# Retention, Mish MLP and GLU on one core: the round's loads are asked for behind a four-byte transfer out of that round's state copy

## The chip, the core and the metric

The kernel runs on one core of one Trainium2 chip. The metric is the device time of one execution in microseconds; the median of several runs is compared.

## What is computed

Three stages follow each other, all in float32. The first is a retention (linear attention with decay) over 2 batches of 768 tokens with 8 heads of 64; the other two are MLPs over the resulting 1536 tokens of width 512.

```python
for t in range(S):
    state = gamma * state + einsum('bhd,bhe->bhde', k[:, :, t], v[:, :, t])
    y[:, :, t] = scale * einsum('bhd,bhde->bhe', q[:, :, t], state)
x = y as (1536, 512)
h = x @ w_in                 # 512 -> 2048
x = (h * tanh(softplus(h))) @ w_out
out = (sigmoid(x @ w_gate) * (x @ w_val)) @ w_out2   # 512 -> 1536 -> 512
```

## The kernel before, in words

The retention is computed in chunks of 128 tokens: six chunks for each of two batches, so 12 rounds (`NSUB`). Each round needs two loads of 512 KB from HBM: `qk_t` (q and k of the chunk, features on the partitions) and `nv_t` (k and v of the chunk, tokens on the partitions). Both come from a pool of four buffers per kind (`AHEAD = 4`, line 774), so a load of a later round waits until the round four before has read its buffer for the last time. `load_qk` and `load_nv` (lines 787 to 795) issue them on SyncE.

From round 5 on, the loop at line 1017 runs `block(j)` (line 934). On TensorE a block holds the state products and half of the scores of round j+1, beside the second half of the outputs of round j-1, then the first half of the outputs of round j with the rest of the scores and of the state of round j+1. Between them stand `keep(j+1, 0)` and `keep(j+1, 1)` (line 860): ScalarE (ACT) copies the running state from PSUM into a tile `s` from a pool of six buffers. The second of them writes `s_t[2 * j + 4]` and is the last thing that `block(j)` issues. `at_prep(j+2)` (line 801) multiplies v by the decay on GpSimd (POOL) into `vp`; it is the first reader of `nv_t` of round j+2. The first reader of `qk_t` of round j+1 are the scores at the start of `block(j)`.

Behind `block(j)` the loop asks for `nv_t` of round j+4 and `qk_t` of round j+3, calls `feed()`, which decodes a weight piece and asks for the next one (`load_piece`, line 356: 512 KB into one of two `raw` buffers, which come free when DVE has decoded them), and then runs a few parts of the first MLP (`work`, line 964) so that TensorE stays busy between blocks. Those are the matmuls `h<-xc`, `hx<-xc`, `h<-B` and `hx<-B` of the trace. In rounds 8 and 9 a `put_block` on ScalarE stands in the middle of the block (line 1016), and in round 8 there is no `feed()`.

In this early part every engine's queue keeps the order in which the program issues (`Queue.issue`, line 143: each instruction is placed after the last one of its engine). SyncE's queue holds all the loads of this part, in order, but for five small tables that ScalarE asks for at the start. After the retention (line 1036 on) a planner, `replay()`, sets the order of the rest from modelled costs; the early part is not in its plan. Because all of it is issued by one helper, nearly all instructions have line 147 in the profile, and they are told apart by their tiles: `sc` scores, `st` state, `ao` outputs of the retention, `s` the state copies, `raw` weight pieces.

Of the kernel before, what the change touches and what calls it, by code (L numbers as in the profile page):

```python
# [9 lines left out]
F32 = mybir.dt.float32  # L10
# [8 lines left out]
P = 128  # L19
# [4 lines left out]
def kernel(ctx, tc, qk, nv, w1i, w1o, w2g, w2v, w2o, ma_in, og_in, sg_in, ck_in, mh_in, out):  # L24
# [12 lines left out]
    NSUB = qk.shape[0]  # L37
# [13 lines left out]
    AHEAD = 4  # L51
# [123 lines left out]
    sync = Queue(nc.sync, lambda n, kw: 1.4 if isinstance(kw["out"], Part) else 1.6, 3.5)  # L175
# [279 lines left out]
    def flush():  # L455
        flush_hi()
        while late_lo:
            late_lo.pop(0)()
        fresh.clear()
# [286 lines left out]
    def run(*parts):  # L746
        for p in parts:
            for s in p:
                s()
# [22 lines left out]
    with ExitStack() as actx:  # L772
        ac = actx.enter_context(tc.tile_pool(name="ac", bufs=1))
# [8 lines left out]
        ck = ac.tile([P, SPB, 2 * NP, 1], F32, name="ck")  # L782
        sg = ac.tile([P, SPB, NP, 1], F32, name="sg")
        og_t = [ac.tile([P, NP, P], F32, name=f"og{b}") for b in range(SPB)]
        qk_t, nv_t, a_t, vp_t, st_t, s_t, sc_t, o_t = {}, {}, {}, {}, {}, {}, {}, {}

        def load_qk(j):
            if j < NSUB:
                qk_t[j] = ld.tile([P, 2, NP, P], F32, tag="qk", name="qk_t")
                sync.dma_start(out=qk_t[j], in_=qk[j])  # L790

        def load_nv(j):
            if j < NSUB:
                nv_t[j] = ld.tile([P, 2, 2 * NP, D], F32, tag="nv", name="nv_t")
                sync.dma_start(out=nv_t[j], in_=nv[j])
# [5 lines left out]
        def at_prep(j):  # L801
            if j >= NSUB:
                return
            vp_t[j] = at3.tile([P, 2 * NP, D], F32, tag="vp", name="vp")
            pool.tensor_tensor(
                out=vp_t[j], in0=nv_t[j][:, 1], in1=ck[:, j % SPB].to_broadcast([P, 2 * NP, D]), op=ALU.mult
            )
            if 0 < j < T:
                decays(j)
# [10 lines left out]
        def scores(j, r):  # L820

            if j >= NSUB:
                return []
            sc, t = ps_h.tile([P, 2, NP, Q], F32, tag="h", name="sc"), qk_t[j]
            sc_t[j, r] = sc

            def pair(p):
                for s in range(2):
                    quarter(sc[rows(s), p // 2, 2 * (p % 2) + (r + p) % 2, :], t[rows(r), 1, p, rows(s)],
                            t[rows(r), 0, p, rows(s)])  # L830

            return [lambda p=p: pair(p) for p in range(NP)]

        def mask(j):
            if j >= NSUB:
                return
            a_t[j] = a = at.tile([P, 2, NP, P], F32, tag="a", name="a")[:, :, :, :Q]
            for r in range(2):
                h = slice(r, NP - r, 3 - 2 * r)
                dve.tensor_tensor(out=a[:, :, h], in0=sc_t.pop((j, r))[:, :, h, :],  # L840
                                  in1=mh.to_broadcast([P, 2, NP // 2, Q]), op=ALU.mult)

        def state(j, s):

            if j >= NSUB:
                return [lambda: [quarter(st_t[0][rows(c), 0, :], z[rows(0), rows(0)], z[rows(0), rows(0)]) for c in range(2)]]
            v, k = vp_t[j], nv_t[j]
            new = j % SPB == 0 and s == 0
            if new:
                st_t[0] = ps_s.tile([P, NP, D], F32, tag="s", name="st")  # L850
            st = st_t[0]

            def pair(p):
                for e in range(2):
                    quarter(st[rows((e + p) % 2), p, :], k[rows(s), 0, 2 * p + e, :], v[rows(s), 2 * p + e, :],
                            new and p == 0, p == NP - 1)

            return [lambda p=p: pair(p) for p in range(NP)]

        def keep(j, s):  # L860
            s_t[2 * j + s + 1] = at6.tile([P, NP, D], F32, tag="s", name="s")
            act.activation(out=s_t[2 * j + s + 1], in_=st_t[0], func=AF.Copy)

        def outs(j, row):

            if not T <= j < NSUB:
                return []
            if row == 0:
                o_t[j] = ps_o.tile([P, NP, P], F32, tag="o", name="ao")
            a, v, t, o = a_t[j], vp_t[j], qk_t[j], o_t[j]  # L870

            def inside(p):
                for e in range(2):
                    quarter(o[rows(e), p, rows(row)], v[rows(row), 2 * p + e, :], a[rows(row), p // 2, 2 * (p % 2) + e, :],
                            row == 0 and p == 0, False)

            def across(p, s):
                for m in range(2):
                    quarter(o[rows((row + m) % 2), p + m, rows(s)], s_t[2 * j + s][rows(row), p + m, :],
                            t[rows(row), 0, p + m, rows(s)], False, True)  # L880

            return [lambda p=p: inside(p) for p in range(NP)] + [
                lambda p=p, s=s: across(p, s) for s in range(2) if (2 * j + s) % (2 * SPB) for p in (0, 2)]
# [44 lines left out]
        def lanes(*sides):  # L928
            for n in range(max(map(len, sides))):
                for side in sides:  # L930
                    if n < len(side):
                        side[n]()

        def block(j, middle=lambda: None):

            lanes(state(j + 1, 0) + scores(j + 1, 0), outs(j - 1, 1))
            if True:
                b = (j - 1) // SPC, (j - 1) % SPC * P
                dve.tensor_tensor(out=acc_t[b[0]][:, :, b[1]:b[1] + P], in0=o_t[j - 1], in1=og_t[(j - 1) % SPB], op=ALU.mult)
            if j == NSUB:  # L940
                return
            keep(j + 1, 0)
            flush()
            at_prep(j + 2)
            middle()
            while late_g:
                late_g.pop(0)()
            if j < NSUB - 1:
                lanes(outs(j, 0), scores(j + 1, 1) + state(j + 1, 1))
                mask(j + 1)  # L950
            else:
                run(outs(j, 0), state(j + 1, 1))
            keep(j + 1, 1)
# [10 lines left out]
        def work(n):  # L964
            for _ in range(n):
                dense.pop(0)()

        def feed():
            pump()
            load_piece()  # L970
# [45 lines left out]
        middles = {2 * SPC: lambda: put_block("B11", 1, 0), 2 * SPC + 1: lambda: put_block("B21", 1, 2)}  # L1016
        for j in range(T + 1, NSUB + 1):
            block(j, middles.get(j, lambda: None))
            load_nv(j + AHEAD)
            load_qk(j + AHEAD - 1)  # L1020
            if j < NSUB and j != 2 * SPC:
                feed()
            if j == NSUB:
                flush()
            for n in range(SHARE[j - T]):
                if j == NSUB:
                    lo_eng["g"] = dve if n > 2 else pool
                    run(late_g)
                    late_g.clear()
                work(1)  # L1030
# [114 lines left out]
```

## Time and profile before

| | |
|---|---|
| median of 3 runs | 580.72 us (578.43 to 580.99) |
| the profiled execution's own time | 578.88 us |
| its span, first to last instruction | 577.0 us |
| TensorE (PE) busy | 568.1 us, 98% of the span |
| VectorE (DVE) busy | 458.9 us, 80% |
| ScalarE (ACT) busy | 294.4 us, 51% |
| GpSimd (POOL) busy | 219.1 us, 38% |
| granted TensorE clock | 1.000 |
| HBM read, written | 48.63 MB, 3.15 MB |
| loads of qk_t and of nv_t | 12 each, 512 KB, 6.7 and 6.8 us to landing (median) |
| loads of raw | 68, 512 KB, 3.2 to 3.4 us to landing (median) |

Shares are of the whole span, and the span has unlike parts: the retention takes the first 66 us, the two MLPs the rest. "Time to landing" runs from the start of a DMA's issue on its queue to the arrival of its last byte's signal. Matmuls overlap in the engine's pipeline, so busy times of TensorE say whether it was ever without work, not how fast it ran.

### The profile page before, as it was taken

What the parts mean: (1) busy time and instruction counts of PE and PEld (TensorE: products, weight loads), DVE (VectorE), ACT (ScalarE), POOL (GpSimd) and SP (SyncE); (2) the same over time, 40 slices, a digit from 0 to 9 for tenths busy, and PEclk for the clock granted to TensorE, in tenths of its full rate; (3) what the DMA queues carried; (4) which work ended last, traced back from release to release, by engine and by line L of the source; (5) the groups of instructions that cost most, each with busy time, mean ns of one, the idle gap of its engine ahead of it and who ended that gap; (6) DMA issues with size and microseconds to landing.
All of it is one profiled execution on the core that took longest, in us unless ns stands there. A gap on an engine that the chain in (4) does not pass through costs nothing.

```text
span 577.0 us, 9810 instructions
## 1 busy us (share of the span) xinstructions
PE 568.1 (98%) x3880; PEld 479.2 (83%) x3880; DVE 458.9 (80%) x680; ACT 294.4 (51%) x544; POOL 219.1 (38%) x198
## 2 busy tenths in 40 slices
PE   8899999999999999999999999999999999999997
PEld 6777888888888888888888878888888888888885
DVE  3877599898998787778988888789888788775574
ACT  1566677585645545355665677545346254231210
POOL 3455588533522300024597554423245043020000
PEclk9999999999999999999999999999999999999999
DMA  9984202422332222112100233221322222000014
GB/s 344 404 294 159 76 0 74 136 86 77 105 110 73 74 73 74 37 39 108 37 1 0 91 128 111 74 87 59 110 74 73 74 73 74 1 0 2 0 38 181
DMA packets 15741, 52.40 MB, mean 91 GB/s; under 512 B 2128, under 2 KB 2256, under 8 KB 15696
## 3 DMA queue, kind: packets, MB, share of 16 engines
q1 hardware_dynamic: 14976, 51.39, 25.5%
q8 instruction: 30, 0.49, 0.3%
q10 hardware_dynamic: 720, 0.40, 0.2%
q14 instruction: 15, 0.12, 0.1%
HBM read 48.63 MB, written 3.15 MB: 90 GB/s over the span
## 4 chain that ended last, share of the span: by engine, by line
PE 95%; DMA 3%; DVE 1%; issue 0%; POOL 0%; SPq 0%; ACT 0%; POOLq 0%; DVEq 0%
PE h L147 37%; PE o L147 37%; PE hx L147 17%; DMA nv_t<-nv 3%; PE ao L147 2%; PE st L147 1%; PE sc L147 1%; DVE h L147 0%; POOL vp L147 0%; SPq L147 0%; DVE acc L147 0%; DVE ww L147 0%; ACT e L147 0%; POOLq L147 0%; DVEq L147 0%
## 5 line engine op out<-in xcount | busy, mean ns | idle before, releaser
L147 PE MATMUL o<-g,wo 128*128 128x512 f32 x492 | 119.1, 391 | 0.0
L147 DVE TENSOR_TENSOR acc<-o,acc 128x512 f32<-128x512 f32 x126 | 86.9, 690 | 39.5 <-PE o L147 37.7
L147 PE MATMUL o<-wo,g 128*128 128x512 f32 x432 | 108.6, 392 | 0.0
L147 PEld LDWEIGHTS o<-g,wo 128*128 128x128 f32 x492 | 90.3, 188 | 17.4
L147 PE MATMUL h<-B,ww 128*128 128x512 f32 x372 | 94.4, 390 | 0.0
L147 PE MATMUL h<-T,ww 128*128 128x512 f32 x366 | 92.9, 390 | 0.1
L147 PEld LDWEIGHTS o<-wo,g 128*128 128x128 f32 x432 | 78.5, 189 | 14.7 <-DVE g L147 0.3
L147 PEld LDWEIGHTS h<-T,ww 128*128 128x128 f32 x366 | 68.4, 188 | 15.1 <-ACT e L147 0.5
L147 PEld LDWEIGHTS h<-B,ww 128*128 128x128 f32 x372 | 68.9, 188 | 13.9
L147 DVE SCALAR_TENSOR_TENSOR raw<-raw 128x512 int32<-128x512 int32 x68 | 61.9, 912 | 2.2 <-ACT raw L147 2.0
L147 ACT ACTIVATE raw<-raw 128x512 int32<-128x512 uint8 x68 | 45.6, 670 | 34.3 <-DMA raw<-w2v 9.1
L147 DVE SCALAR_TENSOR_TENSOR v<-v,raw 128x512 int32<-128x512 int32 x68 | 58.5, 865 | 3.1 <-ACT v L147 0.8
L147 PE MATMUL hx<-xc,ww 128*128 128x256 f32 (+1 forms) x342 | 58.3, 307 | 0.0
L147 POOL TENSOR_TENSOR ww<-s,ww 128x512 fp32r<-128x512 f32 x22 | 30.1, 1371 | 67.8 <-ACT ww L147 67.8
L147 PEld LDWEIGHTS hx<-xc,ww 128*128 128x128 f32 x342 | 50.6, 190 | 5.4 <-DVE ww L147 0.3
L147 POOL TENSOR_TENSOR wo<-v,wo 128x512 fp32r<-128x512 f32 x16 | 21.1, 1330 | 86.2 <-ACT wo L147 49.7
L147 DVE TENSOR_TENSOR h<-h,u 128x512 f32<-128x512 f32 x54 | 37.6, 697 | 15.9 <-PE h L147 14.9
L147 ACT ACTIVATE e<-h 128x512 f32<-128x512 f32 x29 | 17.3, 596 | 59.4 <-PE h L147 48.2
L147 ACT ACTIVATE v<-raw 128x512 f32<-128x512 f32 x68 | 45.1, 666 | 2.1 <-POOL wo L147 1.2
L147 PEld LDWEIGHTS hx<-YT,ww 128*128 128x128 f32 x270 | 38.3, 190 | 3.5
L147 PE MATMUL hx<-YT,ww 128*128 128x256 f32 x270 | 39.4, 282 | 0.0
L147 ACT ACTIVATE g<-h 128x512 fp32r<-128x512 f32 x53 | 31.4, 597 | 14.9 <-DVE h L147 13.9
(97 smaller groups left out, 836.4 us busy)
## 6 DMA issues: line engine op xcount, KB each, us to landing
raw<-w1i SPq DMA_DIRECT2D x16, 512.0 KB, 3.3
raw<-w1o SPq DMA_DIRECT2D x16, 512.0 KB, 3.4
qk_t<-qk SPq DMA_DIRECT2D x12, 512.0 KB, 6.7
nv_t<-nv SPq DMA_DIRECT2D x12, 512.0 KB, 6.8
raw<-w2g SPq DMA_DIRECT2D x12, 512.0 KB, 3.2
raw<-w2v SPq DMA_DIRECT2D x12, 512.0 KB, 3.3
raw<-w2o SPq DMA_DIRECT2D x12, 512.0 KB, 3.3
out<-acc SPq DMA_DIRECT2D x12, 256.0 KB, 2.0
```

Of the source, the lines that this page charges most:

```text
L147: i = call(**kw)
```

## The change

A tile `mark` of 12 floats per partition is added to the pool of the retention. In rounds 5 to 8, ahead of the round's loads, SyncE issues a transfer of one float from the state copy that `block(j)` made last into one column of `mark`. Nothing reads `mark`. SyncE must wait for the copy before it issues that transfer, and its queue keeps order.

```diff
--- before.py
+++ after.py
@@ -782,6 +782,7 @@
         ck = ac.tile([P, SPB, 2 * NP, 1], F32, name="ck")
         sg = ac.tile([P, SPB, NP, 1], F32, name="sg")
         og_t = [ac.tile([P, NP, P], F32, name=f"og{b}") for b in range(SPB)]
+        mark = ac.tile([P, NSUB], F32, name="mark")
         qk_t, nv_t, a_t, vp_t, st_t, s_t, sc_t, o_t = {}, {}, {}, {}, {}, {}, {}, {}
 
         def load_qk(j):
@@ -1016,6 +1017,8 @@
         middles = {2 * SPC: lambda: put_block("B11", 1, 0), 2 * SPC + 1: lambda: put_block("B21", 1, 2)}
         for j in range(T + 1, NSUB + 1):
             block(j, middles.get(j, lambda: None))
+            if j + AHEAD - 1 < NSUB:
+                sync.dma_start(out=mark[:1, j:j + 1], in_=s_t[2 * j + 4][:1, 0, :1])
             load_nv(j + AHEAD)
             load_qk(j + AHEAD - 1)
             if j < NSUB and j != 2 * SPC:
```

## Rows read from the trace of the kernel before

**Rows 1.** Busy time by stretch: us, busy time and instructions by engine, clock, DMA

```profile
28.00:48.00 20.00, 19.47 (x563) 15.15 (x562) 15.34 (x25) 13.31 (x28) 10.29 (x9) 1.00 0.87 305
48.00:66.00 18.00, 17.06 (x376) 14.13 (x376) 12.39 (x17) 11.77 (x24) 8.37 (x7) 1.00 0.31 102
66.00:577.00 511.00, 507.10 (x2523) 429.96 (x2521) 414.83 (x608) 259.92 (x475) 189.00 (x169) 1.00 0.20 66
```

**Rows 2.** The chain of waits from 28 to 66 us, by line, and one piece

```profile
by line: PE hx L147 26.1%; PE h L147 24.8%; PE ao L147 22.0%; PE st L147 12.4%; PE sc L147 7.0%; issue 4.5%; DVE ww L147 2.3%; DVE acc L147 1.2%; DVEq L147 0.1%
...
48.00 0.73 issue
```

**Rows 3.** The timeline of SyncE's queue, 29 to 45 us: start, length, transfer

```profile
29.10 0.33 SPq L147 DMA_DIRECT2D raw<-w1i  x1
29.52 0.38 SPq L147 DMA_DIRECT2D nv_t<-nv  x1
30.00 0.38 SPq L147 DMA_DIRECT2D qk_t<-qk  x1
34.05 0.33 SPq L147 DMA_DIRECT2D raw<-w1o  x1
...
35.30 0.33 SPq L147 DMA_DIRECT2D qk_t<-qk  x1
...
39.63 0.37 SPq L147 DMA_DIRECT2D nv_t<-nv  x1
40.06 0.42 SPq L147 DMA_DIRECT2D qk_t<-qk  x1
...
44.54 0.33 SPq L147 DMA_DIRECT2D qk_t<-qk  x1
```

**Rows 4.** DMA issues in short windows around single requests of rows 3: us to landing

```profile
raw<-w1i SPq DMA_DIRECT2D x1, 512.0 KB, 3.3
...
nv_t<-nv SPq DMA_DIRECT2D x1, 512.0 KB, 5.6
...
qk_t<-qk SPq DMA_DIRECT2D x1, 512.0 KB, 6.4
...
qk_t<-qk SPq DMA_DIRECT2D x1, 512.0 KB, 6.0
...
nv_t<-nv SPq DMA_DIRECT2D x1, 512.0 KB, 6.1
...
qk_t<-qk SPq DMA_DIRECT2D x1, 512.0 KB, 7.0
```

**Rows 5.** The timelines of TensorE and GpSimd: the first readers of the moved loads

```profile
39.05 0.23 PE L147 MATMUL sc<-qk_t 64*64 64x64 f32 x2
...
43.45 0.28 PE L147 MATMUL sc<-qk_t 64*64 64x64 f32 x4
...
48.85 0.27 PE L147 MATMUL sc<-qk_t 64*64 64x64 f32 x2
...
52.96 0.26 PE L147 MATMUL sc<-qk_t 64*64 64x64 f32 x2
...
49.19 1.04 POOL L147 TENSOR_TENSOR vp<-nv_t,ck 128x512 f32<-128x512 f32 x1 [0.83 <-POOL g L147]
```

**Rows 6.** The timeline of ScalarE: the second state copy of rounds 5 to 8

```profile
30.90 0.38 ACT L147 ACTIVATE s<-st 128x256 f32<-128x256 f32 x1 [0.33 <-PE st L147]
...
36.23 0.39 ACT L147 ACTIVATE s<-st 128x256 f32<-128x256 f32 x1
...
40.80 0.38 ACT L147 ACTIVATE s<-st 128x256 f32<-128x256 f32 x1 [0.63 <-PE st L147]
...
46.85 0.36 ACT L147 ACTIVATE s<-st 128x256 f32<-128x256 f32 x1
```

**Rows 7.** What SyncE's queue waited for, 28 to 66 us: us, times, longest

```profile
SPq L147 <- DVE v L147: 55.0, 8, 22.7
```

**Rows 8.** The tile view of qk_t over the whole span: time to landing

```profile
DMA to landing us min/median/max: 3.5/6.7/9.1
```

## The prediction

> **What bounds the kernel now.** I first read the stretches of the span. From 66 us on the attention part is over; TensorE is busy 507.10 of 511 us at full granted clock and the DMA engines are 0.20 busy [rows 1]. Nothing the change touches runs there. The four new transfers belong to rounds 5 to 8, between about 29 and 48 us. In that stretch TensorE is busy 19.47 of 20.00 us and the DMA engines 0.87; in the tail of the attention, 48 to 66, TensorE is busy 17.06 of 18.00 and the DMA engines 0.31 [rows 1]. So TensorE sets the pace there too, and the loads run beside it: heavy traffic, but nobody waits for it.
>
> The second view is the chain of waits over 28 to 66 us. No transfer is on it. What is not TensorE's own work is "issue" with 4.5% of 38 us (1.7 us), DVE ww with 2.3% (0.9 us) and DVE acc with 1.2% (0.5 us) [rows 2]. A change in load times can take time out only by removing part of these 3.0 us, and can add time only by making a load land after its first use. The third reading therefore sets, for each moved load, request, landing and first use side by side [rows 3 to 5].
>
> **The change, part by part.**
>
> *The wait.* SyncE issues in order, so a transfer that waits for the round's second state copy holds back all that follows. The copies end at 30.90+0.38 = 31.28, 36.62, 41.18 and 47.21 us [rows 6]. SyncE reached the same place earlier, at 29.52 in round 5 and at 39.63 in round 7 (round 6 lies between, with its qk request at 35.30), so the wait is real each time [rows 3]. The new transfer's own issue is not in the trace; the other issues take 0.33 to 0.42 us with gaps near 0.1 [rows 3], so I take 0.33 and put the first load 0.5 us behind the copy's end, the second 0.4 behind that. New requests: nv 31.8, 37.1 and 41.7; qk 32.2, 37.5 and 42.1; in round 8, which has no nv load left, qk at 47.7. The seven loads are nv 9 to 11 and qk 8 to 11. The qk requests come 2.2, 2.2, 2.0 and 3.2 us later than 30.00, 35.30, 40.06 and 44.54 [rows 3], the nv requests 2.3 us (29.52) and 2.1 us (39.63) later.
>
> *What else is behind it on SyncE.* The weight loads. They wait for a free raw buffer, that is for the decode on DVE: 55.0 us of waiting over eight requests [rows 7]. The one after round 5 is asked for at 34.05, while the held pair would be out by 32.6; rounds 6 and 7 repeat this. I cost the delay of weight loads at nothing; the cover is DVE's decode, and if that came 1.4 us earlier the weight load would start behind the pair in sequence anyway, as now.
>
> *The four-byte transfer itself.* Nobody reads its target. The state copy's buffer is written again six copies later, so the copy at 46.85 [rows 6] would be the first to wait for the transfer issued at 31.3. Its time to landing is not in the trace: from above I bound it with a whole 512 KB load, 3.3 us [rows 4], so it is done by 35; from below it is nothing. Neither end touches the sum. ACT gets perhaps one more semaphore to test on three copies; ACT idled 0.33 us before one such copy [rows 6], and I take nothing.
>
> *The loads' landing.* Before, request plus time to landing gives qk 36.4 (30.00+6.4), 41.3, 47.1 and 50.5 (6.0 holds for both the second and the fourth), and nv 35.1 (5.6) and 45.7 (6.1) for the first and the last [rows 3, 4]. First uses on TensorE are 39.05, 43.45, 48.85 and 52.96; nv's latest margin is on POOL at 49.19 [rows 5]. The margins are thus 2.6, 2.1, 1.8 and 2.5 us for qk and 3.5 us for the last nv. The two ends:
>
> - Upper end: the delay passes to the landing in full, as if the load took as long as before. qk lands at 38.6, 43.5, 49.1 and 53.7, that is 0.45 us early, then 0.05, 0.25 and 0.75 us late. A late load moves later requests and later uses alike, so these add up to at most 1.05 us.
> - Lower end: a load with nothing in front of it lands 3.3 us after its request [rows 4]. The request at 31.8 then lands at 35.1, where it lands now, and qk 1.3 us behind it (the distance now, 35.1 to 36.4) at 36.4, as now. A transfer asked for later finds less in front of it. Lateness is zero. Below that a gain is possible: traffic that stands clear of other fetches for two microseconds per round could remove stalls without a visible cause, the largest of which is 0.73 us at 48.00 [rows 2]. At most the whole 1.7 us of "issue".
>
> I take the lower end without a gain, because the first pair's landing follows from the nearest row (a weight load of equal size, 3.3 us, in the same stretch at 29.10), and because traffic in the round stage is below full, 0.87 [rows 1], so that a 2 us hole can be refilled.
>
> The rows show landings in the order of requests, with 1.3 to 1.4 us between an nv and its qk [rows 3, 4]. The Trainium skill, in "DMA: Bandwidth & Descriptors", section "Rules for kernel authors", says to issue a transfer early and wait for it late, so that its fixed cost lies beside compute. By that rule the change goes the wrong way and the sum would be the upper end, 1.05 us. The margins above are measured and larger than or nearly equal to the delays, so I let the margins decide.
>
> *Sum:* 0 (wait, covered by 1.8 to 3.5 us of margin) + 0 (weight loads) + 0 (four transfers) = 0 us, with ends at -1.7 and +1.05. The profiled execution took 578.88 us on a span of 577.0; the sum leaves 578.9 there. The median of the three runs is 580.72, 1.8 above, and the runs spread from 578.43 to 580.99. Against the median: 580.7.
>
> **The rivals.**
>
> *Loads become the pace (slower).* If the time to landing were that of the crowded start, up to 9.1 us for qk [rows 8], qk would be needed 6.85, 5.95, 6.75 and 5.25 us after its new request and come 2.25, 3.15, 2.35 and 3.85 us late. Because two rounds overlap, each lateness also relaxes the next deadline: the totals grow 2.25, 3.15, 4.6, 7.0. The price is 7.0 us, 587.7. It decides from a time to landing above 5.3 us in round 8 and 6.0 in round 6. For it: the margins of 1.8 to 2.6 us are about as large as the delay, and TensorE's queue is in order, so that late scores stop everything. Against it: the start is crowded because requests pile up; here the queue is drained when the request comes, so 3.3 to 5 us is more like it. Chance of more than 2.9 us: 0.07.
>
> *Delay passes in full (the upper end).* The load takes as long as before from a later request: 580.7+1.05 = 581.8, no visible difference. For it: the times to landing hardly vary, 5.6 to 7.0 us, whatever was asked before [rows 4]. Against it: those loads each stood behind another one, which the wait undoes. Chance 0.20. (It is also where the skill's rule above would lead; no run here shows it yet.)
>
> *The hole in the traffic pays (faster).* All of the 1.7 us of "issue" going gives 579.0, still within the bound. With DVE ww and acc too (3.0 us) it would be 577.7, 0.5% faster. For it: the 0.73 us stall falls while the queue is loaded. Against it: the held loads are moved into later, equally loaded microseconds, their bytes do not shrink; and DVE's part has no transfer as its releaser. Chance of a visible gain: 0.07; of a gain below it, 0.18.
>
> *The change holds nothing back.* If the copies were done before SyncE arrived, all would stay as it is, 580.7. The rows speak against it in all four rounds. Chance 0.03.
>
> **How the numbers follow.** My forecast, no difference, has 0.45; the upper end 0.20, the small gain 0.18 and the idle change 0.03 also lie within 0.5% (2.9 us, about what a measurement of this kernel can tell from no change). That makes same 0.86, faster 0.07, slower 0.07. The range takes in the small gain and the spread of the runs below (580.7-1.7-1.0 = 578.0) and, above, the late loads with the same 1.0 and a little of the slow rival: 583.0.
>
> **What would show it.** Right: SyncE's nv and qk requests near 31.8/32.2, 37.1/37.5, 41.7/42.1 and 47.7, each about 0.5 us behind the end of a state copy; times to landing of 3.5 to 5 us in place of 5.5 to 7; first scores of the rounds within 1 us of 39.05, 43.45, 48.85 and 52.96; weight requests where they were. Wrong: TensorE idle before scores or POOL idle before vp with a load as the releaser; the last part of the attention, up to 66 us, longer or shorter by over 2 us; or any change in the stretch after 66 us, for which I have no mechanism.

## The result, and the profile after

The change makes the kernel slower. Its median is 584.43 us (581.34 to 587.38, 15 runs) against 580.93 us before (578.43 to 584.16, 15 runs): a ratio of 1.0059, 95% interval 1.0037 to 1.0080. A second measurement of the same two kernels, among the experiments below, gave 1.0039 (1.0022 to 1.0056). No difference was forecast, at 580.7 us in a range of 578.0 to 583.0.

The profiled execution after took 582.36 us on a span of 580.6; the one before 578.88 on 577.0. Both lie near the fast end of their kernel's runs, so they show one part of the difference well and, as will be seen, not all of it.

First the busy time by stretch, after (columns as in [rows 1]).

```profile
28.00:48.00 20.00, 16.85 (x520) 13.31 (x522) 12.51 (x20) 10.82 (x22) 9.25 (x8) 1.00 0.80 261
48.00:66.00 18.00, 16.49 (x390) 13.47 (x379) 13.79 (x21) 12.52 (x26) 8.35 (x6) 1.00 0.36 121
66.00:580.00 514.00, 510.35 (x2567) 432.49 (x2565) 416.09 (x610) 261.59 (x478) 190.43 (x170) 1.00 0.21 67
```

Against [rows 1], TensorE works 16.85 us of the 20 us between 28 and 48, where it worked 19.47. Its totals over the span agree to 0.1 us (568.1 before, 568.2 after), so nothing was added to its work: it stood still. In the stretch from 66 us on it is busy 510.35 of 514 us, as before 507.10 of 511. The clock is 1.00 throughout. The whole loss of this execution arose between 28 and 66 us.

The chain of waits of 28 to 70 us, after, names what stood still.

```profile
by line: PE h L147 24.6%; PE hx L147 23.6%; PE ao L147 19.3%; PE st L147 11.2%; issue 10.9%; PE sc L147 5.5%; DVE ww L147 2.3%; ACT g L147 1.3%; ACT ww L147 1.2%; ACT s L147 0.9%
...
39.28 1.50 issue
...
45.28 1.46 issue
...
49.95 0.29 issue
...
50.92 0.46 issue
...
55.22 0.76 issue
```

"Issue" has 10.9% of 42 us, 4.6 us; before it had 4.5% of 38 us, 1.7 us [rows 2]. Five pieces carry it; the one of 0.29 us stands before too, at 47.03, ahead of the same matmul. No load is on the chain, neither nv nor qk. So TensorE waited for something, at four places, that the profile does not tie to a semaphore, and the difference of 2.9 us is most of the 3.6 us that the span grew.

SyncE's queue, after, is what the prediction asked to see first.

```profile
31.18 0.72 SPq L147 DMA_DIRECT2D mark<-s  x1
32.01 0.34 SPq L147 DMA_DIRECT2D nv_t<-nv  x1
32.45 1.06 SPq L147 DMA_DIRECT2D qk_t<-qk  x1
33.98 0.33 SPq L147 DMA_DIRECT2D raw<-w1o  x1
36.57 0.60 SPq L147 DMA_DIRECT2D mark<-s  x1
37.27 0.33 SPq L147 DMA_DIRECT2D nv_t<-nv  x1
37.70 0.41 SPq L147 DMA_DIRECT2D qk_t<-qk  x1
...
42.77 0.59 SPq L147 DMA_DIRECT2D mark<-s  x1
43.46 0.33 SPq L147 DMA_DIRECT2D nv_t<-nv  x1
43.89 0.39 SPq L147 DMA_DIRECT2D qk_t<-qk  x1
...
50.16 0.58 SPq L147 DMA_DIRECT2D mark<-s  x1
50.84 0.34 SPq L147 DMA_DIRECT2D qk_t<-qk  x1
```

The hold works as intended: the pair of rounds 5 and 6 is asked for at 32.01/32.45 and 37.27/37.70, where 31.8/32.2 and 37.1/37.5 were forecast, and the weight load at 33.98 is where it was [rows 3]. The four-byte transfers take SyncE 0.58 to 0.72 us to issue, where 0.33 was taken. From round 7 on all requests are later than forecast, because TensorE had already stopped at 39.28.

Were the loads late? The times to landing of the four held qk loads, after, in the order of their requests:

```profile
qk_t<-qk SPq DMA_DIRECT2D x1, 512.0 KB, 5.4
...
qk_t<-qk SPq DMA_DIRECT2D x1, 512.0 KB, 6.2
...
qk_t<-qk SPq DMA_DIRECT2D x1, 512.0 KB, 6.6
...
qk_t<-qk SPq DMA_DIRECT2D x1, 512.0 KB, 3.8
```

By request and time to landing they land near 37.9, 43.9, 50.5 and 54.6 us. The rows of TensorE around the first stall, after (start, length, operation, and in brackets the idle time before it):

```profile
38.98 0.23 PE L147 MATMUL sc<-qk_t 64*64 64x64 f32 x2
...
39.06 0.22 PE L147 MATMUL ao<-qk_t,s 64*64 64x64 f32 x1
40.78 0.21 PE L147 MATMUL ao<-qk_t,s 64*64 64x64 f32 x1 [1.50 <-issue]
```

The first scores of round 7's block run at 38.98, over a microsecond after qk had landed, and TensorE then stops for 1.50 us in the middle of a series of like matmuls whose operands are all there. The same in the next two blocks, where the first scores run at 45.00, ahead of the stall, and at 51.50, behind it and 1.0 us after the load:

```profile
45.00 0.28 PE L147 MATMUL sc<-qk_t 64*64 64x64 f32 x4
46.74 0.27 PE L147 MATMUL ao<-qk_t,s 64*64 64x64 f32 x2 [1.46 <-issue]
...
51.37 0.33 PE L147 MATMUL ao<-a,vp 64*64 64x64 f32 x3 [0.46 <-issue]
51.50 0.27 PE L147 MATMUL sc<-qk_t 64*64 64x64 f32 x2
```

What the stalls have in common is their place in the instruction stream. Counted in the trace they lie 254 recorded TensorE instructions apart (matmuls and weight loads), in the kernel before as in the changed one. Before they end at 43.82, 48.73 and 52.79, after at 46.74, 51.37 and 55.98, at the same instructions; the largest one after, which ends at 40.78, has no counterpart before. The chain before, beside the 0.73 us at 48.00 of [rows 2]:

```profile
43.73 0.09 issue
...
52.57 0.21 issue
```

Part 3 of the profile's page shows what comes in such portions: queue 8, kind "instruction", moved 0.49 MB in 30 packets, 16 KB each, and TensorE ran 7760 matmuls and weight loads, 259 for each packet. The Trainium skill, in "Runtime: NRT & Kernel Launch", section "Instruction fetch mechanics", says the same of an engine's program: it is refilled in blocks of 16 KiB, 256 instructions, by DMA. It adds that the cost of such a block's end is mostly hidden; in this stretch the trace does not agree, it costs up to 1.50 us at a time. To keep them apart from the kernel's `block(j)`, these blocks of the program are called portions below; the expectations call them pages, and the DMA engines' queues rings.

The fetch that ends the first stall can be placed with narrow windows. The DMA queues of 36.8 to 37.0 us, before (packets, MB, share of 16 engines):

```profile
q8 instruction: 1, 0.02, 28.7%
```

and of 38.5 to 38.7 us, after:

```profile
q8 instruction: 1, 0.02, 30.6%
```

It is one packet that holds one DMA engine for about 1 us (30.6% of 16 engines over 0.2 us is 0.98 us). Up to 38.9 us TensorE stands at the same instructions in both traces to within 0.1 us, yet the fetch begins at 36.87 before and at 38.58 after, 1.7 us later. It ends at 39.56, and TensorE goes on at 40.78. In all profiles of this study TensorE goes on 1.1 to 1.7 us after such a fetch has ended; where the end of the portion is reached later than that, there is no stall.

### The profile page after: what moved, and what is told of

Its sections match the earlier page's. It is cut to its first block, busy times and chain, and to the rows that moved or that the text cites. A ratio compares the mean times of both kernels' runs of the same rounds, so it can differ in the third digit from the quotient of the medians.

```text
span 580.6 us, 9824 instructions
## 1 busy us (share of the span) xinstructions
PE 568.2 (98%) x3880; PEld 479.2 (83%) x3880; DVE 458.8 (79%) x680; ACT 294.4 (51%) x544; POOL 219.5 (38%) x198
## 4 chain that ended last, share of the span: by engine, by line
PE 94%; DMA 3%; issue 1%; DVE 1%; ACT 0%; ACTq 0%; POOL 0%; POOLq 0%; SPq 0%; DVEq 0%
PE h L147 37%; PE o L147 36%; PE hx L147 17%; DMA nv_t<-nv 2%; PE ao L147 2%; DMA sg<-sg 1%; PE st L147 1%; PE sc L147 0%; DVE h L147 0%; ACTq L147 0%; POOL vp L147 0%; DVE ww L147 0%; DVE acc L147 0%; ACT e L147 0%; ACT g L147 0%
## 5 line engine op out<-in xcount | busy, mean ns | idle before, releaser
L147 ACT ACTIVATE raw<-raw 128x512 int32<-128x512 uint8 x68 | 45.5, 670 | 37.5 <-DMA raw<-w2v 10.7
L147 PEld LDWEIGHTS hx<-xc,ww 128*128 128x128 f32 x342 | 50.5, 190 | 5.4 <-DVE ww L147 0.3
```

The lines of the kernel that those rows point to most:

```text
L147: i = call(**kw)
```

## The experiments

The theory after the first profile: the hold brings the loads into the way of TensorE's instruction fetches (fetch theory). Its rivals: the loads land too late for their readers (late-load theory), and the four-byte transfers themselves disturb (transfer theory). Ratios are to the kernel before, with 95% intervals.

| run | ratio | interval |
|---|---|---|
| e1 transfer behind the first state copy | 1.0001 | 0.9982 to 1.0020 |
| e2 the change, 64 instructions more at the start | 1.0082 | 1.0053 to 1.0111 |
| e3 the change, loads in halves | 1.0107 | 1.0080 to 1.0135 |
| e4 hold in rounds 5 and 6 alone | 1.0013 | 0.9998 to 1.0029 |
| f1 hold in rounds 7 and 8 alone | 1.0030 | 1.0011 to 1.0048 |
| f2 before, 64 instructions more at the start | 1.0054 | 1.0035 to 1.0073 |
| f3 the change, two weight loads one round later | 1.0037 | 1.0015 to 1.0058 |
| f4 before, two weight loads one round later | 0.9978 | 0.9960 to 0.9996 |
| g1 before, 64 instructions more in rounds 1 and 2 | 1.0062 | 1.0046 to 1.0077 |
| g2 the change, the same | 1.0107 | 1.0090 to 1.0124 |
| g3 before, three more loads, no hold | 1.0005 | 0.9991 to 1.0020 |
| g4 as f4, and one part of the MLP earlier | 0.9965 | 0.9949 to 0.9981 |
| h1 the change again | 1.0039 | 1.0022 to 1.0056 |
| h2 hold in round 7 alone | 1.0035 | 1.0016 to 1.0053 |
| h3 the change with the edits of g4 | 1.0034 | 1.0013 to 1.0055 |

**e1: the transfers without the hold.**

```diff
-                sync.dma_start(out=mark[:1, j:j + 1], in_=s_t[2 * j + 4][:1, 0, :1])
+                sync.dma_start(out=mark[:1, j:j + 1], in_=s_t[2 * j + 3][:1, 0, :1])
```

> The four transfers stand where they stand in the change, but read the round's first state copy (ends 29.5, 35.2, 39.7 and 44.1 us in the trace before), so that SyncE is held by 0 to 1 us instead of 2 to 3. Fetch theory (the held loads get in the way of TensorE's instruction fetches, which then come 1.7 to 2.8 us later, and TensorE runs dry): the loads are back within 1 us of their old requests, the stalls called issue between 28 and 66 us fall from 4.6 back to 1.7 to 2.5 us, ratio 0.999 to 1.002. Transfer theory (the four-byte transfers themselves disturb the rings or SyncE): they are all still there, stalls stay near 4.6 us, ratio 1.005 to 1.007.

Measured: 579.97 us, ratio 1.0001. All four transfers are there, only what they wait for comes earlier. The transfer theory falls: four issues and four bytes cost nothing that can be measured. The cost is in the hold. Its profile has 2.4 us of issue between 28 and 70 us (0.63, 0.30, 1.28 and 0.22), the upper end of what was expected. The profiled execution was the slowest of the twelve, 583.40 us, with a stretch at half clock ahead of the rounds, so that its stalls need not be those of the median.

**e4, f1 and h2: which rounds.** The condition ahead of the transfer becomes `j < 7` (e4), `6 < j and j + AHEAD - 1 < NSUB` (f1), or:

```diff
-            if j + AHEAD - 1 < NSUB:
+            if j == 7:
```

> The four-byte transfer in rounds 5 and 6 alone. Fetch theory: the first big stall (1.50 us at 39.3, fetch at 38.6 behind the loads of rounds 5 and 6) stays, the second (1.46 us at 45.3, fetch at 44.3 behind round 7's held pair) goes: ratio 1.002 to 1.004. Late-load theory (round 8 has the least margin, rounds 5 and 6 the most): no loss, 0.999 to 1.001.

> The four-byte transfer in rounds 7 and 8 alone. Rounds 5 and 6 alone cost 0.1%. If the cost sits where the margin of the loads is least and the traffic fullest (both theories): most of the loss, ratio 1.003 to 1.006. If the cost needs the whole row of holds, each pushing the next: 1.001 to 1.003. Fetch theory: the stall of 1.5 us at 39.3 is gone, one of about 1.5 us near 44 to 45 (behind the pair of round 7) stays. Late-load theory: no big stall before 47, then a wait that ends on qk 10 (scores near 48.9).

> The four-byte transfer in round 7 alone. Rounds 7 and 8 cost 0.30%. In their profile the fetch behind round 7's pair came at 51.1 and TensorE stood 2.1 us at 51.5. If that is where the cost sits: ratio 1.002 to 1.004, a stall of 1.5 us or more between 47 and 53 us. If it is round 8's held qk: 0.999 to 1.001.

Measured: 1.0013, 1.0030 and 1.0035. Rounds 5 and 6 cost next to nothing by themselves; the expected stall of 1.5 us at 39.3 did not come in e4's profile, nor one near 44 to 45 in f1's, which has its own of 2.10 us at 51.47. The profiles of e4, f1 and h2 have a stretch at half clock ahead of the rounds, and TensorE comes to round 5 about 3 us later than before; their stalls can't be set place by place against those of the change's first profile. Round 7 alone costs as much as rounds 7 and 8 together, and as much as the whole change in its second measurement. That is neither what the late-load theory says (round 8 has the least margin to its load) nor what the prediction's upper end says (0.25 us for round 7).

The profile of h2 shows how round 7's hold does it. SyncE's queue:

```profile
44.34 0.72 SPq L147 DMA_DIRECT2D mark<-s  x1
45.17 0.34 SPq L147 DMA_DIRECT2D nv_t<-nv  x1
45.60 0.37 SPq L147 DMA_DIRECT2D qk_t<-qk  x1
46.42 0.33 SPq L147 DMA_DIRECT2D raw<-w1o  x1
```

The pair is held to 45.17 and 45.60, until round 7's last state copy, and the weight load follows at 46.42, so that 1.5 MB are asked for within 1.6 us, ahead of the time when TensorE reaches the end of round 8's block, near 48.5 us. The fetch for the next instructions then begins here, in the window 50.9 to 51.1:

```profile
q8 instruction: 1, 0.02, 29.8%
```

and TensorE has its first matmul behind the end of its instructions at 53.24:

```profile
53.24 0.33 PE L147 MATMUL ao<-a,vp 64*64 64x64 f32 x3 [2.10 <-issue]
```

Before, the fetch of the same instructions began 0.9 us after the end of that block (45.4), in the window 46.2 to 46.4:

```profile
q8 instruction: 1, 0.02, 30.2%
```

So the same fetch comes about 2.5 us behind the block's end in place of 0.9, with the same loads in front of it, but asked for later. Round 8's block is followed by one of the two shortest dense pieces (two parts of the first MLP, 1.6 us), so that the next block, 256 recorded instructions in 2 to 3 us, comes soon.

**e2, f2, g1 and g2: the same instructions in other places of their portions.** e2 and f2 add 16 tiny warm-up matmuls, g1 and g2 put as many matmuls of zeros into rounds 1 and 2; e2 and g2 start from the change, f2 and g1 from the kernel before.

```diff
             pe.matmul(out=o, lhsT=z[:, 0:P], rhs=z)
+        for n in range(16):
+            pe.matmul(out=o[:, 0:Q], lhsT=z[:, 0:P], rhs=z[:, 0:Q])
```

```diff
             at_state(j)
+            for n in range(8 if 0 < j < 3 else 0):
+                quarter(st_t[0][rows(0), 0, :], z[rows(0), rows(0)], z[rows(0), rows(0)], False, False)
```

> The change, with 16 more tiny warm-up matmuls at the start of TensorE's queue, 64 instructions, which lie in its idle start. Fetch theory: every page of 256 instructions ends 64 instructions earlier in the program, so the stalls leave the places where they stand now (after the second to fourth retention outputs of the blocks of rounds 7 and 8) and reappear 64 instructions earlier, in front of the blocks or in their first state products; their sizes change, because the fetches meet other loads: ratio anywhere between 0.998 and 1.008. Late-load theory (TensorE waits for qk or nv that come too late): the stalls stand before the same matmuls as now, ratio 1.005 to 1.007.

> The kernel before, with the same 16 tiny warm-up matmuls (64 instructions). Fetch theory: its small stalls (0.73 us at 48.00, 0.21 at 52.57, 0.09 at 43.73) go from their places and come 64 instructions earlier or nowhere; no hold, so no load is late: ratio 0.997 to 1.002, and the loss of the change against it is the late loads' part. If the warm-up itself costs (2 us at the start that are not hidden): 1.002 to 1.004.

> The kernel before, with 16 tiny matmuls that add zeros to the state (64 TensorE instructions) in rounds 1 and 2, where the start waits for its loads anyway. The same shift of the page ends as with the longer warm-up, without its start cost of about 1 us. Fetch theory: the small stalls leave 48.00 and 52.57; from the run with the longer warm-up one of 1.7 us is to be expected near 46 to 47, in the dense matmuls: ratio 1.001 to 1.005. If the position of the instructions in their pages does not matter: 0.999 to 1.001.

> The change with the same 64 instructions in rounds 1 and 2. Fetch theory: the stalls of 1.5 us at 39.3 and 45.3 go, others come, as with the longer warm-up: ratio to before 1.004 to 1.009. Late-load theory (the position in the pages does not matter): stalls as in the change, 1.005 to 1.007, before the same matmuls.

Measured: 1.0082, 1.0054, 1.0062 and 1.0107. The two stalls of the change at 39.3 and 45.3 are gone in e2, as the fetch theory says, and its largest one, 2.59 us at 50.91, stands 64 instructions ahead of the place of the change's stall at 55.22, among the last products of round 9's block (chain of waits):

```profile
50.91 2.59 issue
```

In f2 the stall of the kernel before at 48.00 has moved to 46.98, into the dense matmuls, with 1.72 us; g1 and g2 stop at that same instruction, for 2.05 us (at 49.05) and 3.09 us (at 50.38). The position of the instructions in their portions decides where TensorE stops; the late-load theory has no room for that. But the times are no clean measure, and all four lie above what was expected, e2 by very little: the 64 instructions were not hidden. In f2 the rounds begin about 1 to 2 us later than before, in g1 about 3 us (the weight load of 29.10 is asked for at 31.01 and at 32.12), a large part of what these kernels lose (3.1 and 3.6 us). What can be read from the pairs is the hold's price on other bases: 0.3% between f2 and e2, which their intervals do not clear of zero, and 0.45% between g1 and g2, which theirs do.

e2 also shows how a late load appears in a trace. TensorE's row in round 9's block:

```profile
49.29 0.27 PE L147 MATMUL sc<-qk_t 64*64 64x64 f32 x2 [0.87 <-DMA qk_t<-qk]
```

Here the wait ends on qk itself and the profile says so: 0.87 us. In the two profiles of the change no such row exists. The late-load theory names a limit that is close by, about 1 us away, but not the one that was met.

**e3: loads in halves.**

```diff
-                sync.dma_start(out=qk_t[j], in_=qk[j])
+                for h in halves(j):
+                    sync.dma_start(out=qk_t[j][h], in_=qk[j][h])
...
-        sync.dma_start(out=t, in_=src[kind][i])
+        for h in ((slice(0, Q), slice(Q, P)) if early and n > 2 else (slice(0, P),)):
+            sync.dma_start(out=t[h, :], in_=src[kind][i][h])
```

`nv` is treated as `qk`; `halves(j)` gives two halves of 64 partitions from chunk 8 on.

> The change, with the loads of rounds 5 on (nv and qk from chunk 8, raw from piece 3, in the early part) asked for as two halves of 64 partitions. Fetch theory, if a fetch waits for the share of whole transfers in front of it: half the wait, the stalls called issue fall from 4.6 to 2 to 3 us, ratio 1.001 to 1.004. If a fetch waits for all that is asked for: no change, 1.005 to 1.007. Late-load theory: more issues on SyncE (0.33 us each), later landings, 1.006 to 1.010.

Measured: 1.0107, a miss for the fetch theory's first form. Stalls of 2.24 us (at 53.40) and 1.12 us remain, and a wait for qk joins them. Counted from 128 recorded instructions ahead of the portion's end, a mark that all traces share, the fetches for the places of the change's first three stalls began after 2.2, 2.8 and 3.9 us, against 3.1, 2.5 and 1.4 us in the change's first profile: on the whole they did not get their turn sooner behind shorter transfers. But e3 also doubles the issues on SyncE, so its time is not the halves' effect on fetches alone. What a fetch waits for, whether all that has been asked for or something else, stays open. The Trainium skill, in "DMA: Bandwidth & Descriptors", section "Queues, rings and completion order", says that each DMA engine takes turns between its queues packet by packet; by that rule, if one transfer's share of an engine makes a packet, halves should have helped, and they did not.

**f3, f4, g4 and h3: less traffic in the same stretch.** The weight loads of rounds 6 and 7 are asked for one round later (f3 on the change, f4 on the kernel before). g4 and h3 also move one part of the first MLP from behind round 11 to behind round 9.

```diff
-            if j < NSUB and j != 2 * SPC:
-                feed()
+            if j == T + 2:
+                pump()
+            elif j == 2 * SPC:
+                load_piece()
+            elif j < NSUB:
+                feed()
```

```diff
-    SHARE = (4, 4, 3, 3, 2, 2, 4, 5, 5)
+    SHARE = (4, 4, 3, 3, 2, 3, 4, 4, 5)
```

> The change, with the weight loads of rounds 6 and 7 asked for one round later (behind the loads of rounds 7 and 8; they are decoded at 50.8 and 55.8 us in the trace before, so they have the time). One transfer of 512 KB less between 39 and 48 us. Theory that full rings behind the held pair delay fetches and qk: ratio 1.002 to 1.004, qk 9 and 10 land 1 us or more sooner after their request (5 us or less instead of 6.2 and 6.6), the stall at 45.3 shrinks below 1 us, the one at 39.3 stays. If the hold costs by itself, whatever the traffic: 1.005 to 1.007.

> The kernel before, with the weight loads of rounds 6 and 7 asked for one round later. If TensorE's stalls between 43 and 53 us (1.0 us in all) come from full rings: they halve, ratio 0.997 to 0.999. If they do not depend on the traffic: 1.000. If the later weight pieces come too late for the decode: 1.001 to 1.004.

> The kernel before with the weight loads of rounds 6 and 7 one round later (0.998 by itself) and one part of the first MLP moved from behind round 11 to behind round 9, so that TensorE has dense work while a fetch is under way. Fetch theory: the stall near 52 to 54 (0.3 to 0.7 us) goes too: ratio 0.996 to 0.999. If the moved part only shifts work: 0.998, as without it.

> The change with the weight loads of rounds 6 and 7 one round later and one part of the first MLP moved from behind round 11 to behind round 9 (0.9965 without the hold). If the hold's cost is the fetches behind the held pairs: it stays about 0.5% above that kernel, 1.000 to 1.004, with a stall near 50 us. If thin traffic makes up for the hold: 0.996 to 0.999.

Measured: 1.0037, 0.9978, 0.9965 and 1.0034. Thinner traffic makes the kernel before 0.2% faster. With the hold it shows no clear gain: f3's 1.0037 stands against 1.0059 and 1.0039 for the change, and its profile has 2.38 us of stall at 50.00 and none at 39.3, where one was expected to stay. With the MLP part g4 is the fastest kernel of the study, 578.82 us against 581.22 on its chip. Its chain between 28 and 70 us:

```profile
by line: PE h L147 33.6%; PE hx L147 24.6%; PE ao L147 17.1%; PE st L147 11.9%; PE sc L147 5.7%; issue 2.6%; POOL og L147 2.4%; DVE ww L147 2.2%; DVE acc L147 1.1%; POOLq L147 0.1%
...
43.87 0.26 issue
...
47.33 0.30 issue
...
52.49 0.30 issue
```

Issue is down to 2.6% of 42 us, 1.1 us, and the 0.73 us at 48.00 [rows 2] is gone. The hold keeps its price: 0.6% between f4 and f3, 0.7% between g4 and h3. h3's profile still has stalls of 1.08 and 1.17 us (at 44.52 and 54.77; near 50, where one was expected, it has 0.46). So the traffic of the two weight loads is not what makes the hold dear; what is left is the time at which the pair is asked for.

**g3: more traffic without a hold.**

```diff
             load_qk(j + AHEAD - 1)
+            if j < 2 * T:
+                sync.dma_start(out=acc_t[2][:, 0:2, :], in_=qk[j].rearrange("p a b c -> p a (b c)"))
```

> The kernel before, with one more load of 512 KB behind the pair in rounds 5 to 7 (three in all; it writes a part of the accumulator that is overwritten later, so it adds traffic only). No load is held. Fetch theory: TensorE's stalls at the ends of its pages grow (1.0 us in all between 43 and 53 us before) to 3 us or more, though the pairs are asked for when they were: ratio 1.003 to 1.010. Late-load theory: TensorE waits at the scores for qk, and the chain shows the load as releaser: 1.002 to 1.008. If neither the fetches nor the loads are near their limit: 0.999 to 1.001.

Measured: 1.0005, no difference, although its profile shows what the fetch theory expects:

```profile
by line: PE hx L147 24.6%; PE h L147 23.4%; PE ao L147 20.2%; issue 11.9%; PE st L147 11.2%; PE sc L147 6.4%; DVE ww L147 2.5%; DVE acc L147 1.1%; DVEq L147 0.1%
...
39.70 1.43 issue
...
45.62 1.25 issue
...
51.05 1.28 issue
```

With no load held, three more loads on the DMA engines put TensorE's stalls at the same three instructions as in the change, 1.43, 1.25 and 1.28 us, with no load as releaser. That supports the mechanism. The ratio does not follow, a miss: 4 us of stalls in one profile, and 0.05% in the medians. Two things lie between. The first is that the stalls differ from run to run. Five profiles, of kernels without added matmuls, have no stretch at half clock up to 570 us: before, after, g3, g4 and h3. Their spans are 577.0, 580.6, 580.4, 576.3 and 579.8 us, their "issue" between 28 and 70 us is 1.7, 4.6, 5.0, 1.1 and 3.4 us, and the span less this issue is 575.2 to 576.4 us in all five. By this estimate an execution at full clock is slower by about as much as its stalls are longer. So the profile before, 578.88 us, shows less stall time than the median of its kernel has, and that of g3, the second slowest of its twelve runs (582.23 us against a median of 581.44), shows more. At full clock the medians of g3 and of the kernel before on its chip are 581.2 and 580.7 us, a difference that is not clear of noise. The second is that ten of the twelve runs of g3 are at full clock, which leads to the last question.

**h1: the change again, with the clock of every run.** No edit.

> The change, unaltered, to see a second profile and the clock of every run of both kernels on one chip. If the loss is only the stalls that the first profile shows at full clock (4.6 us of issue against 1.7): the runs at full clock of both kernels differ by 3 to 3.5 us, and lower clocks are as frequent in both. If stalls also bring the clock down: runs at full clock differ by 1 to 2.5 us, most runs of the change are below full clock and a third or fewer of those of before, and a profile at a lower clock shows the fall right behind a stall of 2 us or more near 50 us. Ratio 1.004 to 1.008.

Measured: 582.27 us against 580.41, ratio 1.0039. The second expectation holds in part. The mean granted clock of a run tells two groups apart. Of the kernel before, over the experiments, 81 of 109 runs had full clock (mean 0.999 or 1.000, median 580.21 us) and 28 less (582.21 us). Of the change, both measurements together, 9 of 27 had full clock (582.06 us) and 18 less (584.3 us). On h1's chip alone it is 7 of 12 against 24 of 28, with 582.06 against 580.23 us at full clock: the 1.8 us lie where they were expected, but most runs of the change have full clock there.

A run's loss thus has two parts. At full clock the change is 1.8 us slower: the stalls. And two thirds of its runs instead of a quarter are below full clock. These runs are 2.0 to 2.3 us slower than the others of their kernel, which makes about 0.9 us on average (0.41 times 2.2). Together 2.7 us, 0.47%, between the two ratios measured. The second part is less certain than the first. A mean clock does not say where the clock fell: the profiles of e4 and f4 have 0.994 from a stretch near 23 to 30 us alone, ahead of everything the change touches, and f1 and h2 have 0.991 from such a stretch and a later one. Nine of the change's 27 runs are at 0.991 or less. How much of the 0.9 us is the change's doing, and how much of the 2.0 to 2.3 us is the clock and not longer stalls, is not shown.

h1's profile shows a fall behind a stall. Its chain between 28 and 70 us has 2.4 us of issue, as much as e1's, and of the first profile's stalls at 39.28 and 45.28 only 0.42 us of the second are left:

```profile
by line: PE h L147 27.4%; PE hx L147 25.5%; PE ao L147 20.9%; PE st L147 12.6%; PE sc L147 8.1%; issue 5.8%
...
44.01 0.42 issue
...
48.61 1.55 issue
```

It is the fastest of its twelve runs, 581.55 us, so the 4.6 us of the first profile are no fixed amount. TensorE's row behind the stall, and the stretches around it (columns as in [rows 1]):

```profile
50.16 0.33 PE L147 MATMUL ao<-a,vp 64*64 64x64 f32 x3 [1.55 <-issue]
```

```profile
47.00:50.40 3.40, 1.56 (x40) 1.00 (x42) 1.52 (x4) 3.07 (x8) 1.34 (x1) 1.00 0.65 243
50.40:53.80 3.40, 3.40 (x100) 3.19 (x98) 1.35 (x3) 0.89 (x3) 3.17 (x3) 0.50 0.21 75
53.80:57.00 3.20, 3.20 (x134) 2.64 (x133) 2.79 (x3) 1.44 (x4) 1.58 (x2) 1.00 0.03 5
```

TensorE stood for 1.55 us up to 50.16, in a stretch in which it was busy 1.56 of 3.40 us, and from 50.4 to 53.8 the granted clock is 0.50, 1.2 GHz in place of 2.4. Pairs of its score matmuls start every 0.11 us there, and every 0.06 us in the same block before. Of the profiles of this study, those of e3, f1, f2, f3, g1, g2, h1 and h2 have such a stretch of low clock between 49 and 60 us, each behind a stall of 1.1 to 3.1 us (in g2 it begins 0.5 us before the stall's end); e2 has a stall of 2.59 us and no fall. The profiles of before, of the change's first measurement, e1, e4, f4, g3, g4 and h3, whose stalls are 1.5 us or less, have none there. Several profiles, with a hold and without, have another stretch at 0.50 near 23 to 31 us, ahead of everything the change touches.

## Why the prediction was wrong

*What bounds the kernel.* It said that TensorE sets the pace in the rounds and that nobody waits for the traffic. The first half holds. The second was wrong: TensorE's own instructions come through the same DMA engines, and their fetches were already behind its pace at 43.73, 48.00 and 52.57 us. The 1.7 us of "issue" was on the list [rows 2], but only as something that could be saved.

*The wait and the requests.* Right to 0.3 us for rounds 5 and 6. The issue of a four-byte transfer was mis-sized, 0.58 to 0.72 us and not 0.33, without consequence.

*Weight loads and the four transfers at nothing.* Right for the transfers, shown by e1. The weight requests of rounds 5 and 6 stayed where they were (33.98 and 39.13).

*The landing.* The first nv took the 3.3 us of the lower end, but the times to landing of 3.5 to 5 us were wrong for the first three qk, where 5.4, 6.2 and 6.6 us were measured. Even so they landed 1.1, 1.1 and 1.0 us ahead of their first readers in the first profile, so the sum's term of zero for late loads held there. The rule that was weighed, to issue a transfer early, gave the right sign for a reason other than the one it names: no load was late, no fixed cost was uncovered.

*The step that failed* is "Lower end ... Below that a gain is possible". The hold was allowed to change the stalls in one direction only. It makes them larger: 4.6 us against 1.7 in the first pair of profiles, 2.4 in the change's second one, 1.8 us on the median at full clock. With it fell the statement that the upper end of the sum is 1.05 us, and the range's upper end with it. The sum also had no term for the granted clock, which was 1.000 in the one profile it went by; 18 of 27 runs of the change were below full clock.

*The rivals.* None of the four was the case. "Loads become the pace" has the right sign, at 7.0 us where 3.5 were measured; its mechanism, scores waiting for qk, is seen in e2 and e3 and not in the change. "The hole in the traffic pays" had the right object, the 0.73 us stall at a loaded time, and the wrong sign.

*What was to show it.* The first scores of the rounds ran 0, 1.6, 2.7 and 3.2 us later than before, and the stretch up to 66 us ended over 2 us later, which had been named as a sign of error. What had not been named is a stall without a releaser.

## What to carry to other kernels

Look at "issue" in the chain before moving transfers: where an engine runs hundreds of tiny instructions in a few microseconds, its instruction fetches are a load like any other, with a deadline that no semaphore shows, and they share the DMA engines with the data. Asking for data later can bring a burst in front of such a fetch even though every load still lands in time; compare the time at which the fetch begins, not only the landings. One profile is one draw: here the size of the stalls and the clock behind them differ from run to run, and only the clocks of many runs showed how often it falls.

## What was not expected of the hardware

Where TensorE stands at the end of a portion, it goes on 1.1 to 1.7 us after its instruction packet has ended, in every profile, whatever ran beside it. In g4 one fetch began 0.13 us after TensorE had started the instruction that is 128 recorded ones ahead of the portion's end (45.06 and 45.19 us), with the DMA engines 0.33 busy just before. Counted from the same point it was 1.3 to 1.6 us in rounds 5 to 8 before the change, and 3.1 and 2.5 us ahead of the change's two large stalls; in other traces some fetches begin ahead of that point (51.46 against 51.79 us in h1). And eight of the nine profiles with a stall of 1.55 us or more in the rounds have a stretch of 3.4 us or more at half clock that begins within 1.5 us of the stall's end. What exactly a fetch waits for, and why three additional loads that lengthen the stalls as much as the hold in one profile hardly move the median, is not settled.
